# Rows of small matmuls joined in a delta-rule attention and SiLU feed-forward kernel

## The chip, the cores and the metric

The kernel runs on one core of a Trainium2 chip. The metric is the device time of one execution in microseconds (us). Engines: PE (matrix multiply; its weight loads are listed apart as PEld), DVE (vector), ACT (scalar, activations), POOL (general), SP (issues most of the DMAs). Each runs its own queue of instructions in order and waits on semaphores of the others.

## The reference

32 heads (4 batches x 8 heads) of 768 tokens and 48 features go through a delta-rule recurrence; the result, 3,072 tokens of 384 features, goes through a feed-forward block with SiLU.

```
k_n = k / (norm(k) + 1e-6)
state = zeros(48, 48)                       # per batch and head
for t in range(768):
    y[t] = q[t] @ state
    state += beta[t] * outer(k_n[t], v[t] - k_n[t] @ state)
x = y, heads side by side                   # (3072, 384)
h = x @ w_in                                # w_in (384, 2048), given in 64 bits
out = (h * sigmoid(h)) @ w_out              # w_out (2048, 384), given in 64 bits
```

## The kernel before

The tokens are cut into six chunks of 128, c = 0 to 5. Inside a chunk the recurrence is solved as a triangular system per head. For a chunk the work falls into three stages, written as Python generators that are stepped by hand:

- `prepare(c)` (L1431): scale v by the lengths of the keys (`size`, POOL), turn k and q so that their features lie on partitions, then `score(c, b, ...)` for the four batches b. The keys of chunk 2 are turned by `turn` (L501): PE transposes into PSUM (`pt`), DVE copies out. Those of the later chunks and all queries are turned by DVE alone (`turn_blocks`, L489). A score (L530, tile `pa`) is 16 matmuls that write two PSUM banks, of which ACT copies one part and DVE masks the other. After every second score `block_out` has SP store the diagonal blocks of 32x32 to memory (L104, `blocks`), and `block_in` loads them back with one system on each partition.
- `invert(c, step)` (L617 on): DVE inverts the blocks in 31 rounds of two instructions (`rank`, `x`; L628 and L633). `step`, the step size of each token, is made ahead of it by `block_steps` (L442 on): one matmul (`pg`, L446) and an ACT copy. For chunks 2 to 5 the result takes a way through memory and comes back as `xe` and `xi`. For chunk 1 `put_up` (L602) lays it out on the chip instead: two 32x32-block transposes by DVE (into `xe_y` and `up`) and copies of `up` into `xi` and `crossed` by all three engines.
- `solve(c)` (L975): the first merge (L783, `py`, 64 matmuls of 32x32 blocks for both groups of batches), the first keys (L829, `ph`, 32 matmuls), the second merge (`px`), then for each half of the chunk inner and old (L841 and L909), update (L861, `pu`), new (L922, `pyc`), copies of the result to `xT` by ACT, and DMAs (`move`, L902) for those parts that change partition. The second half begins with keys of its own.

Each matmul of the program stands as two PE and two PEld instructions in the profile, a transpose as one of each.

Between these small steps PE works on the feed-forward block of the chunk before. `feed_forward(c, hf)` is also a generator: 16 pieces of `hidden` (L1044, `phid`, six matmul instructions each) and 14 of `combine` (L1151, eight each) for each half of a chunk; chunk 0 has `project` (L1079, `po`) in place of combine. `run(n)` (L1411) takes n such pieces, `go(steps, n)` (L106) n steps of a stage, and `together` (L110) drives several parts matmul by matmul. The order of PE's instructions is the order in which these calls are made; `pin` chains the instructions of every engine in that order. SP's DMAs stand in one line in order of the calls too.

Two places hold the order around the change. Up to the solving of chunk 1 it is a text of words (L1541): s is a step of `solve`, r is `run`, p a step of `prepare(1)`, g makes the step sizes of chunk 1 and the generator of its inversion, i is a round of the inversion, z is a `size` of chunk 1, v loads its v, l and m are steps of the lengths of chunks 1 and 2, f and b narrow the 64-bit weights, t sums weights. From there on it is the loop at L1544: solve chunk c with pieces between its steps, prepare chunk c + 1, invert it with some 23 pieces among its 32 rounds, and take some pieces more.

Of the kernel before, what the change touches and what calls it, by code (L numbers as in the profile page):

```python
# [19 lines left out]
def kernel(  # L20
# [59 lines left out]
    def pin(op):  # L80

        engine = op.ins.engine
        if engine in pins:
            behind(op, pins[engine])
        pins[engine] = op
        return op
# [19 lines left out]
    def go(steps, n=1):  # L106
        for _ in range(n):
            next(steps, None)
# [493 lines left out]
    def put_up(x):  # L602

        both = work.tile([P, BH, T], FP32, name="xe_y", tag="g", bufs=1)
        xes[1], ys[1] = both[:], both[:].rearrange("p (g h) t -> p g h t", g=2)
        pin(nc.vector.transpose(out=both[:].rearrange("p n s -> p s n"), in_=x))
        up = work.tile([P, BH, T], FP32, name="up_1", tag="x", bufs=1)[:]
        pin(nc.vector.transpose(out=up.rearrange("p n t -> p t n"), in_=x.rearrange("p s t -> p t s")))
        for j in (1, 3, 0, 2):
            rows, cols = slice(T * j, T * (j + 1)), slice(T * (j % 2), T * (j % 2) + T)  # L610
            for g in range(2):
                of = up[rows, HH * g : HH * (g + 1)]
                if j % 2 == 1 and g == 1:
                    by_act(crossed[T * (4 - j) : T * (5 - j)], of)
                (by_dve if j % 2 == 1 and g == 0 else by_pool if j % 2 == 0 and g == 0 else by_act)(xis[g][rows, :, cols], of)
# [359 lines left out]
    def solve(c):  # L975

        if c == 0:
            together(inner(0, 0, 0, CC))
            together(inner(0, 1, 0, M))
            yield  # L980
            first_outputs(0)
            yield
            first_outputs(1)
            yield
            together(update(0, 0, 0), update(0, 1, 0))
            yield
            together(keys(0, 0, 1), keys(0, 1, 1))
            yield
            together(inner(0, 0, 1), old(0, 0, 1))
            yield  # L990
            together(inner(0, 1, 1), old(0, 1, 1))
            yield
            together(update(0, 0, 1), update(0, 1, 1))
            yield
            together(new(0, 0, 1), new(0, 1, 1))
            copy_out()
            copy_out()
            move()
            yield
            return  # L1000
        together(merge(c, 0, False), merge(c, 1, False))
        yield
        together(keys(c, 0, 0), keys(c, 1, 0))
        yield
        together(merge(c, 0, True), merge(c, 1, True))
        yield
        for hf in range(2):
            if hf == 1:
                together(keys(c, 0, 1), keys(c, 1, 1))
                if c > 1:  # L1010
                    follow(c)
                yield
            for g in range(2):
                together(inner(c, g, hf), old(c, g, hf))
            if hf == 1:
                if c == 1:
                    follow(c)
                load_v(c + 1)
            yield
            made(c, hf)  # L1020
            yield
            copy_out()
            move()
            if hf == 0:
                yield
# [405 lines left out]
    def prepare(c):  # L1431

        def evacuate(j, e, to, of):
            if j == 1:
                mask(to, of)
            else:
                by_act(to, of)

        def scored(b):
            if b == 0:  # L1440
                block_room(c)
            score(c, b, (0, 1), (A, CC), evacuate)
            if b % HB == 1:
                block_out(c, b // HB)

        if in_blocks(c):
            for g in range(2):
                size(c, g)
            if c == 2:
                for b in range(B):  # L1450
                    turn(c, b, 0, (A, CC)[b % 2], True)
            for g in range(2):
                for b in range(HB * g, HB * (g + 1)):
                    turn_blocks(c, b, 1)
                if g == 1:
                    for b in range(HB):
                        scored(b)
                yield
            for b in range(HB, B):
                scored(b)  # L1460
            block_in(c)
            yield
            return
        block_room(1)
        for b in range(B):
            score(1, b, (0,), (CC, CC), evacuate)
            if b % HB == 1:
                block_out(1, b // HB)
            yield
        block_in(1)  # L1470
        yield
        for b in range(B):
            score(1, b, (1,), (A, CC), evacuate)
            yield
# [63 lines left out]
                pieces = chained(feed_forward(1, 0), feed_forward(1, 1))  # L1538

    for text in (  # L1540
        "s f s f T f q T s q T j5 j4 j8 j8 f j5 f q r T j20 j5 j8 j4 j16 j5 j4 b r q r f j4 j4 f W7 r b j4 f2 j4 j4 j32 r f e j6 j6 b j8 j4 f j4 j20 f j4 r j4 j99 l h f2 b l s w2 f r2 l2 p r s w3 r p r l p f l2 f l3 b l f l2 s l f l p l3 r l3 s l f l r l2 p f s2 l2 f l4 f r2 f p2 v l g r i p i p f r i r i2 r i r i b l i r f r i r b r2 i b b b i2 r2 i2 f b i5 r6 f r f r i2 r2 f r i r f r f i4 f i b r2 i3 b f b f r i r i f k r f r z i b r s r2 t z s b r2 b s m2 r5 t f t m f t m2 r s t m r b s b m r m2 s r m r m r c m2 s m r m t b m2 s m2 b m f m2 t r t m3 r m s m",  # L1541
    ):
        script(text)
    for c in range(1, NCH):  # L1544
        if c > 1:
            solving = solve(c)
            for n in range(9):
                go(solving)
                run(((2, 2, 2, 2, 1, 1, 2, 2, 2), (2, 2, 2, 1, 1, 2, 2, 2, 2))[c == NCH - 1][n])
                if n == 5:  # L1550
                    pieces = chained(pieces, feed_forward(c, 0), feed_forward(c, 1))
        assert next(solving, 0) == 0
        go(long_2, 99)
        if c + 1 < NCH:
            ready = prepare(c + 1)
            go(ready)
            run(2)
            step = block_steps(c + 1)
            for _ in ready:
                run(2)  # L1560
            run(6)
            for n, _ in enumerate(invert(c + 1, step)):
                run(int(n % 4 != 3 and n != 24))
                if n == 3:
                    load_k(c + 2)
                    if in_blocks(c + 2):
                        load_blocks(k, c + 2, ALL)
            after = lengths(c + 2) if c + 2 < NCH else iter(())
            for _ in range({1: 8, NCH - 2: 10}.get(c, 10)):
                run()  # L1570
                go(after, 4)
            go(after, 99)
# [31 lines left out]
```

## Time and profile before

| | us |
|---|---|
| median of 3 runs | 645.06 |
| lowest, highest | 644.01, 648.04 |
| the profiled execution | 643.82 |
| its span, from the first to the last instruction | 642.1 |
| PE busy | 621.8 |
| DVE busy | 404.7 |
| ACT busy | 216.8 |
| POOL busy | 94.8 |

The mean granted clock of PE was 0.978 of full speed. The page cuts the span into 40 slices of 16 us and gives the busy share of each in tenths; the chain of waits is the work that ended last, followed back from the end; "issue" is time in which an engine waited for nothing that the profile shows. A row of a group reads: line, engine, operation, tile written <- tiles read, shapes, count | busy us, mean ns of one | idle us just before them. A row of the timeline reads: start, duration, engine, line, operation, count, and in brackets the idle time before it with what ended it. A row of windows reads: stretch, its length, then for each engine the busy us with the number of instructions, the granted clock, the share of the DMA engines and GB/s.

Large matmuls of the feed-forward block fill most of PE's time: L1044 has 258.5 us, and L1151 has five groups of 28 to 57 us each on the page.

### The profile page before, as it was taken

The page shows a single profiled execution, that of the slowest core. Times are in us where ns is not written, and L with a number is a line of the kernel's source. Part 1 is how long each engine was busy: PE and PEld are TensorE (multiplying, and loading weights), DVE is VectorE, ACT ScalarE, POOL GpSimd, SP SyncE. Part 2 cuts the span into 40 slices and gives each one's busy share as a digit, 9 for nine tenths or more (in the row PEclk, how much of TensorE's full clock was granted, in tenths as well). Part 3 has the DMA queues.
Part 4 walks back from the last instruction along what each step waited for, and adds up shares of the span by engine and source line. Part 5 has one row for each costly group of instructions (what it writes and reads, how often), then busy time and mean ns, then how long its engine had stood idle before and what let it go on. Part 6 is the DMA issues. An engine that isn't in the chain of part 4 may idle for free.

```text
span 642.1 us, 21892 instructions
## 1 busy us (share of the span) xinstructions
PE 621.8 (97%) x9642; PEld 546.6 (85%) x9642; DVE 404.7 (63%) x917; ACT 216.8 (34%) x512; POOL 94.8 (15%) x96
## 2 busy tenths in 40 slices
PE   6879999999999999999999999999999999999997
PEld 4778778666689989989989989989989989889997
DVE  5846879998775974755975554976565963212112
ACT  2656674152251122441122351122451122441120
POOL 5323531255020020020020020020010000000000
PEclk9759999999999999999999999999999999999999
DMA  9756354260469241469142359332163033100101
GB/s 189 168 152 195 109 125 98 74 125 3 101 128 168 43 89 21 86 122 155 39 94 31 75 121 162 57 82 31 46 140 70 22 74 41 40 13 1 26 0 26
DMA packets 141695, 53.69 MB, mean 84 GB/s; under 512 B 113296, under 2 KB 135056, under 8 KB 141600
## 3 DMA queue, kind: packets, MB, share of 16 engines
q1 hardware_dynamic: 141264, 52.14, 39.9%
q8 instruction: 76, 1.25, 0.8%
q10 hardware_dynamic: 336, 0.15, 0.1%
q14 instruction: 19, 0.16, 0.1%
HBM read 39.62 MB, written 10.49 MB: 78 GB/s over the span
## 4 chain that ended last, share of the span: by engine, by line
PE 70%; DVE 10%; DMA 8%; SPq 7%; issue 2%; ACT 1%; POOL 1%; POOLq 0%; DVEq 0%
PE phid L1044 27%; PE px L1151 13%; PE py L1151 10%; PE po L1079 7%; DVE rank L628 4%; DVE x L633 3%; PE pz L841 2%; PE pa L530 2%; SPq L197 2%; PE ph L829 2%; PE pyc L909 2%; SPq L142 1%; PE pyc L922 1%; DVE sums_of_g L1133 1%; DMA up<-x 1%
## 5 line engine op out<-in xcount | busy, mean ns | idle before, releaser
L1044 PE MATMUL phid<-xT,w_in 128*128 128x256 f32 x1152 | 258.5, 382 | 1.0 <-DMA xT<-part 0.9
L1044 PEld LDWEIGHTS phid<-xT,w_in 128*128 128x128 f32 x1152 | 215.8, 190 | 32.0 <-issue 3.0
L1054 ACT ACTIVATE gT<-phid 128x512 f32<-128x512 f32 x88 | 52.5, 598 | 142.2 <-PE phid L1044 137.6
L628 DVE SCALAR_TENSOR_TENSOR rank<-g,step,x 128x31 f32<-128x31 f32 (+15 forms) x124 | 49.7, 401 | 36.5 <-DMA g<-blocks 33.0
L1133 DVE TENSOR_TENSOR sums_of_g<-gT 128x384 f32<-128x384 f32 (+1 forms) x60 | 30.4, 525 | 57.2 <-ACT gT L1054 46.6
L1151 PE MATMUL py<-w_out,sums_of_g 128*128 128x192 f32 x320 | 56.8, 329 | 0.0
L1151 PE MATMUL px<-sums_of_w,sums_of_g 128*128 128x192 f32 x320 | 56.6, 329 | 0.0
L1151 PEld LDWEIGHTS px<-sums_of_w,sums_of_g 128*128 128x128 f32 x320 | 52.2, 190 | 0.5
L1151 PEld LDWEIGHTS py<-w_out,sums_of_g 128*128 128x128 f32 x320 | 52.2, 190 | 0.4
L633 DVE TENSOR_TENSOR x<-x,rank 128x31 f32<-128x31 f32 (+15 forms) x124 | 42.5, 342 | 4.3
L468 POOL TENSOR_TENSOR vf<-vf,n_slot 128x768 f32<-128x768 f32 x10 | 15.2, 1524 | 173.3 <-DMA vf<-in_v_dram 173.3
L868 DVE TENSOR_TENSOR state<-state,pu 48x384 f32<-48x384 f32 x44 | 24.3, 552 | 21.4 <-PE pu L861 20.4
L545 ACT COPY xT<-pyc 48x128 f32<-48x128 f32 (+2 forms) x126 | 32.6, 259 | 1.6
L489 DVE STREAM_TRANSPOSE kq<-stage 128x512 f32<-128x512 f32 x28 | 28.4, 1112 | 5.9 <-DMA stage<-in_q_dram 5.8
L1151 PE MATMUL py<-w_out,gT 128*128 128x192 f32 x160 | 28.4, 329 | 0.0
L1151 PE MATMUL px<-sums_of_w,gT 128*128 128x192 f32 x160 | 28.4, 329 | 0.0
L1151 PE MATMUL px<-w_out,gT 128*128 128x192 f32 x160 | 28.0, 327 | 0.0
L841 PEld LDWEIGHTS pz<-vf,xi 64*64 64x64 f32 x768 | 25.0, 142 | 3.2 <-issue 2.6
L551 POOL COPY g<-x 64x256 f32<-64x256 f32 x4 | 5.0, 1238 | 152.3 <-DVE x L636 152.3
L1151 PEld LDWEIGHTS px<-w_out,gT 128*128 128x128 f32 x160 | 26.4, 190 | 0.5
L841 PE MATMUL pz<-vf,xi 64*64 64x48 f32 x768 | 26.6, 226 | 0.0
L1151 PEld LDWEIGHTS py<-w_out,gT 128*128 128x128 f32 x160 | 26.1, 190 | 0.3
(197 smaller groups left out, 832.3 us busy)
## 6 DMA issues: line engine op xcount, KB each, us to landing
vf<-in_v_dram SPq DMA_DIRECT2D x48, 96.0 KB, 2.9
out_dram<-o SPq DMA_DIRECT2D x42, 96.0 KB, 2.2
w_out<-in_moe_w_in_dram SPq DMA_DIRECT2D x12, 256.0 KB, 3.3
sums_of_w<-in_moe_w_out_dram SPq DMA_DIRECT2D x8, 384.0 KB, 3.6
blocks<-ap SPq DMA_DIRECT2D x40, 64.0 KB, 1.9
g<-blocks SPq DMA_DIRECT2D x5, 512.0 KB, 3.6
kb<-in_k_dram SPq DMA_DIRECT2D x12, 192.0 KB, 4.4
kb<-in_k_dram SPq DMA_DIRECT2D x24, 96.0 KB, 4.5
```

Of the source, the lines that this page charges most:

```text
L468: pin(nc.gpsimd.tensor_tensor(out=vf, in0=vf, in1=of, op=ALU.mult))
L489: pin(nc.vector.transpose(out=kqs[c, b][:, :, j, :].rearrange("p a (i m) -> p a m i", i=T), in_=src.rearrange("p a (m d) -> p a m d", d=D) ...
L545: return pin(nc.scalar.copy(to, of))
L628: pin(nc.vector.scalar_tensor_tensor(out=tv, in0=g[:, 0:m, m : m + 1].to_broadcast([P, m, n]), scalar=step[:, m : m + 1], in1=x[:, m : m + ...
L633: yield pin(nc.vector.tensor_tensor(out=x[:, 0:m, m:T], in0=x[:, 0:m, m:T], in1=tv, op=ALU.add))
L841: yield pin(nc.tensor.matmul(pz[rows, n * D : (n + 1) * D], lhsT=xis[g][rows, u * H + 2 * p + e, :], rhs=vfs[c][rows, hf, g * HB + u, p, : ...
L868: pin(nc.vector.tensor_tensor(out=to, in0=to, in1=by_heads(pu[of]), op=ALU.add))
L1044: pin(nc.tensor.matmul(ph[:, j * GT : (j + 1) * GT], lhsT=w_in[:, a, (2 * f + j) * P : (2 * f + j + 1) * P], rhs=xTs[c, hf][:, a, :], star ...
L1054: pin(nc.scalar.activation(out=hidden_of(c, hf, f), in_=ph[:], func=ACTF.Silu, scale=-0.5 if in_blocks(c) else 0.5))
L1079: pin(nc.tensor.matmul(pos[i][:, 0:DM], lhsT=hidden_of(0, hf, f // 2)[:, at : at + C], rhs=w_outs[f // HFF][:, f % HFF, :], start=(f == 0) ...
L1133: pin(nc.vector.tensor_tensor(out=sums_of_g[:, k, fs], in0=of[0], in1=of[1], op=op))
L1151: pin(nc.tensor.matmul(to, lhsT=at, rhs=quarter(f, *b) if isinstance(b, tuple) else sums_of_w[b][:, f], start=start and f == 0, stop=f == ...
```

## The change

Five edits, all of them in order or layout; no arithmetic is added or taken away.

1. `put_up` (chunk 1): the two transposes write their results without a stride, so that the order of the axes in `xe` and `up` is another; the merge's reads of `xe` and the copies' reads of `up` now have a stride of 32 elements.
2. `solve`: no step ends between the first merge and the first keys. They are issued together, and the loops over `solve` have one step fewer (8, not 9).
3. `prepare` for chunks 2 to 5: the scores of all four batches come in one step, not in two pairs. For chunk 2 a step ends before its keys are turned, so that two pieces come first.
4. In the text for chunk 1: v, l and g (load v, lengths, step sizes) stand ahead of two p (scores), and the second z ahead of the s that holds the first merge.
5. The number of pieces: in the solving of a chunk 2, 2, 2, 1, 1, 2, 2, 2 for all of chunks 2 to 5; after the scores 8; after the inversion 12 (8 where chunk 2 is inverted).

```diff
     def put_up(x):
 
         both = work.tile([P, BH, T], FP32, name="xe_y", tag="g", bufs=1)
-        xes[1], ys[1] = both[:], both[:].rearrange("p (g h) t -> p g h t", g=2)
-        pin(nc.vector.transpose(out=both[:].rearrange("p n s -> p s n"), in_=x))
-        up = work.tile([P, BH, T], FP32, name="up_1", tag="x", bufs=1)[:]
-        pin(nc.vector.transpose(out=up.rearrange("p n t -> p t n"), in_=x.rearrange("p s t -> p t s")))
+        turned = both[:].rearrange("p n t -> p (n t)").rearrange("p (s n) -> p s n", s=T)
+        xes[1], ys[1] = turned.rearrange("p s n -> p n s"), both[:].rearrange("p (g h) t -> p g h t", g=2)
+        pin(nc.vector.transpose(out=turned, in_=x))
+        up = work.tile([P, T, BH], FP32, name="up_1", tag="x", bufs=1)[:]
+        pin(nc.vector.transpose(out=up, in_=x.rearrange("p s t -> p t s")))
...
-                of = up[rows, HH * g : HH * (g + 1)]
+                of = up[rows, :, HH * g : HH * (g + 1)].rearrange("p t n -> p n t")
...
         together(merge(c, 0, False), merge(c, 1, False))
-        yield
         together(keys(c, 0, 0), keys(c, 1, 0))
         yield
...
             if c == 2:
+                yield
                 for b in range(B):
                     turn(c, b, 0, (A, CC)[b % 2], True)
             for g in range(2):
                 for b in range(HB * g, HB * (g + 1)):
                     turn_blocks(c, b, 1)
-                if g == 1:
-                    for b in range(HB):
-                        scored(b)
                 yield
-            for b in range(HB, B):
+            for b in range(B):
                 scored(b)
             block_in(c)
             yield
```

In the text the words around the two places are (before, then after):

```diff
-f r2 f p2 v l g r i p i p f r
+f r2 f v l g p2 r i p i p f r
...
-f r z i b r s r2 t z s b r2 b s m2
+f r z i b r z r2 s t b r2 b s m2
```

And the loop:

```diff
         if c > 1:
             solving = solve(c)
-            for n in range(9):
+            for n in range(8):
                 go(solving)
-                run(((2, 2, 2, 2, 1, 1, 2, 2, 2), (2, 2, 2, 1, 1, 2, 2, 2, 2))[c == NCH - 1][n])
-                if n == 5:
+                run((2, 2, 2, 1, 1, 2, 2, 2)[n])
+                if n == 4:
                     pieces = chained(pieces, feed_forward(c, 0), feed_forward(c, 1))
...
             ready = prepare(c + 1)
+            for _ in range(3 if c == 1 else 2):
+                go(ready)
+                run(2)
+            step = block_steps(c + 1)
             go(ready)
-            run(2)
-            step = block_steps(c + 1)
-            for _ in ready:
-                run(2)
-            run(6)
+            run(8)
...
-            for _ in range({1: 8, NCH - 2: 10}.get(c, 10)):
+            for _ in range(8 if c == 1 else 12):
                 run()
                 go(after, 4)
```

## What I predict

> **What bounds the kernel now.** I read the page first (busy shares, the 40 slices), then the chain of waits in order of time, then the waits of PE, last the DMA queues and counts by window.
>
> ```profile
> PE 621.8 (97%) x9642; PEld 546.6 (85%) x9642; DVE 404.7 (63%) x917; ACT 216.8 (34%) x512; POOL 94.8 (15%) x96
> PE   6879999999999999999999999999999999999997
> PEclk9759999999999999999999999999999999999999
> ```
>
> PE is busy for 621.8 of 642.1 us, at 9 tenths from the fifth slice on and at the full granted clock. The 20 us that it idles lie almost all in the first 50 us, which the change does not touch. So time after that can come from three things only: the cost of each matmul, what PE pays when it goes from one kind of matmul to another, and the few stalls left. The matmuls stay the same ones; only their order changes.
>
> What a switch costs stands in the chain (start, us, what):
>
> ```profile
> 342.33 1.50 PE px L1151 x8
> 343.83 1.30 PE py L1151 x8
> ...
> 451.14 0.86 PE pu L861 x64
> 452.00 0.90 PE pyc L922 x64
> ...
> 563.46 1.04 PE pyc L922 x64
> ...
> 434.43 1.22 PE py L783 x82
> ...
> 438.45 1.08 PE ph L829 x64
> ...
> 471.65 1.91 PE pa L530 x64
> ...
> 476.34 1.91 PE pa L530 x64
> ```
>
> The same eight large matmuls take 1.50 us behind a block of small ones and 1.30 behind large ones: going back costs 0.20. The block "new" (pyc L922) takes 0.90 behind another small block and 1.04 behind large matmuls: going in costs 0.14. The scores (pa L530) take 1.91 both behind the small pg and behind large matmuls, so for them going in costs nothing.
>
> The stalls that PE has in the steady part, each with its releaser in brackets (timeline; the two group rows are of the first merge: chunks 2 to 5, then chunk 1):
>
> ```profile
> 157.74 0.49 PE L922 MATMUL pyc<-ap,z 64*48 64x64 f32 x18 [0.26 <-issue]
> 176.53 0.71 PE L501 MATMUL pt<-ident,kb 128*128 128x128 f32 x5 [0.98 <-issue]
> 341.30 1.03 PE L829 MATMUL ph<-state,kq 48*64 48x48 f32 x56 [0.22 <-issue]
> 548.03 0.33 PE L861 MATMUL pu<-z,kb 64*48 64x48 f32 x10 [0.23 <-issue]
> ...
> L783 PE MATMUL py<-xe,ap 32*32 32x32 f32 x512 | 5.6, 193 | 0.2
> L783 PE MATMUL py<-xe_y,ap 32*32 32x32 f32 x128 | 1.3, 193 | 0.0
> ```
>
> Four of them end with "issue": PE waited for no engine and no transfer. They are the key to this change. Between them lie these numbers of instructions (window, its length, then PE and PEld busy with counts):
>
> ```profile
> q8 instruction: 76, 1.25, 0.8%
> ...
> 157.74:176.53 18.79, 17.81 (x382) 12.93 (x382) 14.40 (x42) 6.80 (x18) 0.00 (x0) 1.00 0.37 87
> 176.53:341.30 164.77, 164.14 (x2033) 150.01 (x2033) 116.29 (x287) 47.42 (x118) 17.07 (x18) 1.00 0.54 95
> 341.30:548.03 206.73, 206.50 (x3306) 189.68 (x3305) 129.89 (x291) 62.00 (x159) 14.00 (x14) 1.00 0.37 72
> ```
>
> One queue carries 76 packets of instructions; PE's 2 x 9642 instructions divided by 76 are 254 a packet. The distances between the stalls are 764, 4,066 and 6,611 instructions: 3 x 254.7, 16 x 254.1 and 26 x 254.3. So PE stalls where a new packet begins, and it does so because the packet isn't there yet. How long a packet takes to come is bounded by the time that the last 254 instructions or so before each stall took:
>
> ```profile
> 154.20:157.73 3.53, 3.27 (x131) 2.26 (x122) 3.24 (x7) 0.53 (x2) 1.48 (x1) 1.00 0.03 5
> 173.50:176.52 3.02, 2.05 (x130) 1.84 (x130) 1.99 (x4) 1.09 (x3) 0.00 (x0) 1.00 0.76 170
> 337.10:341.29 4.19, 3.98 (x132) 3.62 (x118) 3.87 (x15) 1.15 (x2) 0.00 (x0) 1.00 1.06 106
> 544.50:548.02 3.52, 3.29 (x133) 2.90 (x124) 0.00 (x0) 1.34 (x4) 0.00 (x0) 1.00 0.02 5
> ```
>
> 3.0 to 4.2 us, mean 3.6: wherever PE runs through a packet faster than that, it waits for the next. Large matmuls use 16 instructions in 1.3 us and never do. A first merge is 256 instructions in 1.22 us and keys are 128 in 1.08; it is the 2.8 us of large matmuls between them that lets the supply keep up.
>
> **The change part by part.**
>
> *Rows joined.* In chunks 1 to 5 the first merge and the first keys stand together, in chunks 2 to 5 the two pairs of scores. Nine times PE saves going back, 9 x 0.20 = 1.8 us; five times (keys behind the merge) also going in, 5 x 0.14 = 0.7. Sum 2.5 us gained. The row of 0.90 has two blocks of one tile shape behind each other, while a merge has tiles of 32 rows and keys tiles of 48; no row shows that pair, so the term's ends are 2.5 and 1.8 (going back alone), and I take 2.5. [...] What bears on four scores in a row:
>
> ```profile
> 282.33 0.65 ACT L545 COPY ap<-pa 128x256 f32<-128x256 f32 x2 [0.45 <-PE pa L530]
> ...
> 188.14 0.65 ACT L545 COPY ap<-pa 128x256 f32<-128x256 f32 x2 [0.23 <-PE pa L530]
> ...
> 189.51 2.67 SPq L104 DMA_DIRECT2D blocks<-ap  x5
> ```
>
> A score's PSUM banks are used again by the third score behind it; ACT clears them in 0.65 us (two copies) while PE takes 1.91 / 2 = 0.96 for a score, so I cost that at nothing, up to 0.5 a row if an older instruction of ACT or DVE is ahead.
>
> *Stalls that go.* Chunk 2's turned keys (pt) come two pieces later. The packet stall of 0.98 falls there, straight behind update and new; with 2.8 us of large matmuls ahead it goes, for one more switch (0.34): 0.64 gained. Against that, 2.8 us more lie ahead of the scores; the pieces run from the last score to the first merge stay 39 for chunk 2 (8 + 23 + 8) and become 43 in place of 41 for chunks 3 to 5 (the last term 12, not 10). First merges wait today: 5.6 + 0.2 - 4 x 1.3 = 0.6 us over four chunks, for xe. For chunks 3 to 5 two pieces more (2.6 us) hide that; for chunk 2 SP is what sets it (behind the loads of q and v and the moves it comes to the block stores at 189.51, when ACT has cleared the last score at 188.79), and that time stays while the merge comes later. 0.6 gained. In the last chunk two pieces, not one, now stand between inner and update: the 0.23 at 548.03 goes. The 0.22 at 341.30 goes into the next part. Sum 1.7 us gained.
>
> *Waits that come.* In the last chunk one piece fewer stands between "new" and the first hidden of the same chunk:
>
> ```profile
> 549.39 0.56 ACT part L545
> ...
> 553.57 3.56 DMA xT<-part
> ...
> 557.26 1.41 PE L1044 MATMUL phid<-xT,w_in 128*128 128x256 f32 x4 [0.85 <-DMA xT<-part]
> ```
>
> ACT, SP and the DMA need from 549.39 to 557.13 whatever PE does, and PE waits already: one piece of 1.30 less is 1.3 lost. At chunk 1 the step sizes (pg) go ahead of two scores:
>
> ```profile
> 90.24 1.61 ACT L545 COPY xT<-pyc 48x128 f32<-48x128 f32 x6
> 91.91 0.41 PE L446 MATMUL pg<-pick,spread 128*128 128x32 f32 x2 [0.69 <-ACT xT L545]
> ```
>
> pg waits there for a PSUM bank that ACT clears at 91.85. In the new order the second score gets that bank; it is reached at about 91 and the rest of its work comes behind the wait, so 0.3 is lost (ends: 0.7 gained, 0.7 lost). Chunk 1's put_up writes its two turned tiles without a stride and reads them with one. DVE's rows for the same 1,024 elements:
>
> ```profile
> L606 DVE STREAM_TRANSPOSE xe_y<-sums_of_w 128x1024 f32<-128x1024 f32 x1 | 2.0, 2036 | 0.0
> L1294 DVE STREAM_TRANSPOSE sums_of_w<-blocks 128x1024 f32<-128x1024 f32 x1 | 1.2, 1249 | 0.0
> ```
>
> L1294 writes without a stride, so two of them save some 1.5 us of DVE. PE's merge of chunk 1 does not wait (1.3 above) and now comes 2.6 us later, behind two more pieces of large matmuls, so this is worth nothing; a slower strided read of xe by PE costs between 0 and 1.3 (that merge twice as long), and I take 0. Sum 1.6 us lost.
>
> *The packets.* The boundaries lie 254 instructions apart and can be carried from the stalls to the new rows, since both programs have run the same instructions when the first keys of chunks 2 to 5 end. Counts up to those ends:
>
> ```profile
> 176.53:244.36 67.83, 67.49 (x640) 61.38 (x639) 52.57 (x133) 18.19 (x43) 8.59 (x9) 1.00 0.62 106
> 341.30:342.32 1.02, 1.02 (x57) 0.96 (x56) 0.54 (x1) 0.00 (x0) 0.00 (x0) 1.00 0.01 1
> 341.30:439.44 98.14, 98.14 (x1506) 90.16 (x1505) 64.75 (x155) 29.61 (x76) 8.43 (x9) 1.00 0.47 87
> 536.66:548.02 11.36, 11.13 (x353) 10.25 (x350) 5.02 (x10) 3.15 (x8) 0.00 (x0) 1.00 0.02 4
> ```
>
> Chunk 2: 1,279 instructions are 5 packets of 254 and 9 more: one boundary 9 before the end of the keys, the one ahead of it 134 before the end of the merge. Between them 134/256 of 1.22 and 119/128 of 1.08: 1.65 us where 3.6 are needed, so 1.95 lost. Chunk 5: 703 forward to a boundary, three packets (762) back: one 59 before the end of the keys, the other 185 before the end of the merge; 0.88 + 0.58 = 1.46, so 2.1 lost. Chunk 3: one 113 before the end of the keys, the other 239 before the end of the merge, 1.27 us apart; but that first boundary lies only 17 instructions into the merge, and if the sequencer runs that far ahead of PE, its packet is asked for while large matmuls still run. Ends 0.2 (today's stall at this very boundary) and 2.3; I take 0.3, as today's packet, asked for 50 instructions into the merge (254 less 32 large and 16 of the keys leave 206 of its 256), came 0.22 late only. Chunk 4: boundaries 87 before the end of the merge, then 39 behind the keys, then 5 behind the second merge; the first distance takes 0.4 + 1.1 + 2.8 = 4.3, enough, the second 1.2, but the sequencer may enter it earlier: between 0 and 2.4, I take 0.7. Chunk 1's boundaries lie as in chunk 4 with longer pieces: 0. A row of scores is 256 instructions in 3.8 us: 0. Sum 5.1 us lost (ends 3.0, with packets in 3.0 us and nothing in chunks 3 and 4, and 9.5, with 4.2).
>
> *The sum.* -2.5 - 1.7 + 1.6 + 5.1 = +2.5 us. The profiled execution took 643.82 (642.1 of span and 1.7 around it), so 646.3. That run lies 1.2 under the median of 645.06, inside the spread of the three (644.01 to 648.04); I predict **646.3** and let the range carry the difference.
>
> **The rivals.** *The supply keeps up* (25%): in the new order packets are asked for far enough ahead, and only the mean of small and large matters. Against it: four stalls at whole packets. For it: these four cost 1.7 us in all, and today's rows of update and new are 256 instructions in 1.8 us and stall rarely. Time: 643.82 - 2.5 - 1.7 + 1.6 = 641.2. *Every row starves* (7%), the side of slower: packets take 4.2 us or more whenever PE takes small matmuls without a break, so each of five merge-and-keys rows loses 2.5 and each of four score rows 0.5, with 0.4 for what follows each of the nine: 12.5 + 2.0 + 3.6 = 18.1 in place of 5.1, 659.3; it decides from about 10 us of packet stalls on, at which the whole is over 1% slower. [...]
>
> **How the numbers follow.** 60% for the forecast, whose own range is 643.8 to 649.5 (the packets' ends in part, the pg bank, the run-to-run spread). From 641.2 less some noise of a run to the strided case and some starving: 640.3 to 650.5 for eight in ten. A measurement of this kernel can tell about 1%, 6.5 us. Faster by more than that (under 638.6) needs the first rival and all gains at their ends: 0.03. Slower (over 651.5): starving, and a little of the strided case: 0.09. Within 1%: 0.88.
>
> **What would show it.** New PE stalls that end with "issue", near 2 us each, inside the first keys of chunks 2 and 5, and none of that length in chunk 1; the 0.98 ahead of pt gone; phid in the last chunk waiting about 2.2 us for xT; runs of 1.50 us fewer by nine. If the keys run through in 1.1 us behind the merge everywhere, the packet term is wrong and the first rival holds; if scores stall too, the second.

## The result and the profile after

The changed kernel takes 655.92 us (median of 6 runs, 655.35 to 657.32) where the kernel before, timed beside it, takes 646.09 (6 runs, 644.01 to 648.23): a ratio of 1.0153, 95% interval 1.0124 to 1.0182. It is 9.8 us slower, 9.6 above the forecast and 5.4 above the upper end of the range. The profiled execution took 655.94 with a span of 654.1.

The page of the changed kernel, in its rows for PE and its clock:

```profile
span 654.1 us, 21891 instructions
...
PE 627.6 (96%) x9642; PEld 554.4 (85%) x9642; DVE 404.0 (62%) x917; ACT 220.1 (34%) x512; POOL 95.6 (15%) x96
...
PE   6879999999999998999999999999999998899997
...
PEclk8759999999999997999999999999999998899999
```

The span grew by 12.0. PE has the same 9,642 instructions, yet is busy for 5.8 us more, and idle for 6.2 more. Idle time was forecast; that the same instructions take longer was not. The clock row tells where: a 7 in slice 16 and 8s in slices 34 and 35, where before stood 9s.

Not all of the 12.0 belongs to the change. Before the first product of the last projection of chunk 0 (`po`) stand some 115 us in which loading and start-up vary from kernel to kernel, also where nothing was edited: in the experiments that do not add instructions there, the first `po` comes between 115.37 and 120.60. Of the change, only the first move of edit 4 (loads, lengths and step sizes of chunk 1) lies ahead of it: scores (pa) wait there for ACT for 1.02 + 0.35 us where pg waited 0.69 before, 0.7 more. The forecast had 0.3 for that, 0.7 at its end. The timeline has that first `po` before, then after the change:

```profile
115.62 1.76 PE L1079 MATMUL po<-w_out,gT 128*128 128x384 f32 x4
```

```profile
118.24 0.81 PE L1079 MATMUL po<-w_out,gT 128*128 128x384 f32 x2
```

From there to the end it is 642.1 - 115.6 = 526.5 before and 654.1 - 118.2 = 535.9 after: 9.4 us. This stretch, called the rest below, is compared in the experiments; everything that the change does from chunk 1's first merge on lies in it. Each "rest" comes from the one execution that was profiled. PE's busy time in it, before and after (windows):

```profile
115.62:642.11 526.49, 519.97 (x7161) 461.31 (x7159) 317.50 (x711) 152.90 (x375) 52.09 (x46) 1.00 0.37 70
118.24:654.14 535.90, 524.43 (x7161) 467.65 (x7159) 316.61 (x710) 155.86 (x375) 52.87 (x46) 0.99 0.36 69
```

So of the 9.4 us, 4.5 are longer busy time and 4.9 are idle time.

The timeline of PE in the first keys of chunk 2, then of chunk 5 (start, us, what, idle time before it with its releaser):

```profile
243.60 0.25 PE L784 MATMUL py<-xe,ap 32*32 32x32 f32 x4
244.37 1.25 PE L784 MATMUL py<-xe,ap 32*32 32x32 f32 x124 [0.51 <-DMA xe<-low]
245.55 1.13 PE L830 MATMUL ph<-state,kq 48*64 48x48 f32 x61
249.15 0.45 PE L830 MATMUL ph<-state,kq 48*64 48x48 f32 x3 [2.46 <-issue]
...
541.44 0.78 PE L830 MATMUL ph<-state,kq 48*64 48x48 f32 x35
544.26 0.76 PE L830 MATMUL ph<-state,kq 48*64 48x48 f32 x29 [2.04 <-issue]
```

The two stalls stand where the packet count had put them, in those two rows and with about that length (1.95 and 2.1 were forecast). What follows them is new. Windows of the changed kernel (length, PE and PEld busy with counts, DVE, ACT, POOL, then the granted clock, DMA share, GB/s):

```profile
243.50:249.15 5.65, 2.65 (x191) 2.30 (x190) 5.14 (x18) 1.16 (x2) 0.00 (x0) 0.88 1.07 122
249.15:255.00 5.85, 5.85 (x44) 5.48 (x47) 1.02 (x2) 0.06 (x1) 0.00 (x0) 0.54 0.02 3
255.00:262.00 7.00, 7.00 (x278) 6.68 (x264) 2.91 (x5) 2.93 (x7) 0.00 (x0) 1.00 0.02 5
...
544.30:550.50 6.20, 6.20 (x173) 5.84 (x173) 2.47 (x5) 0.33 (x1) 0.00 (x0) 0.72 0.01 3
...
565.50:569.50 4.00, 2.35 (x6) 1.00 (x6) 0.63 (x2) 0.17 (x1) 0.00 (x0) 0.89 0.36 86
569.50:572.70 3.20, 3.20 (x130) 3.13 (x129) 0.00 (x0) 0.53 (x2) 0.00 (x0) 0.61 0.28 67
```

Behind each standstill PE runs without a gap, but at 0.54, 0.72 and 0.61 of its clock in the mean of these windows. Length times missing clock is 5.85 x 0.46 + 6.20 x 0.28 + 3.20 x 0.39 = 2.7 + 1.7 + 1.2 = 5.6 us, and up to 0.4 more in the window ahead of the third (0.89). That is more than half of the 9.4. It is also more than the 4.5 of longer busy time, because the joined rows save more busy time than chunk 1 (below) pays. The loss in the third of these windows stands behind the waits of the last chunk's first hidden for xT:

```profile
565.98 0.67 PE L1044 MATMUL phid<-xT,w_in 128*128 128x256 f32 x2 [0.67 <-DMA xT<-part]
567.02 0.67 PE L1044 MATMUL phid<-xT,w_in 128*128 128x256 f32 x2 [0.38 <-DMA xT<-part]
568.49 1.10 PE L1044 MATMUL phid<-xT,w_in 128*128 128x256 f32 x2 [0.80 <-DMA xT<-part]
```

Chunk 1 pays as well. Groups of the changed kernel (busy us, mean ns | idle): the merge of chunk 1 and three of the copies of `up`:

```profile
L784 PE MATMUL py<-xe_y,ap 32*32 32x32 f32 x128 | 2.0, 228 | 0.0
...
L545 ACT COPY xi<-up 32x512 f32<-32x512 f32 x4 | 4.3, 1073 | 0.0
...
L551 POOL COPY xi<-up 32x512 f32<-32x512 f32 x2 | 2.8, 1402 | 0.1
L548 DVE COPY xi<-up 32x512 f32<-32x512 f32 x2 | 2.3, 1132 | 0.1
```

Reading with a stride makes the merge 2.0 instead of 1.3 us; the copies, by the same group rows before, took 616 (ACT), 776 (POOL) and 570 ns (DVE).

### The profile page after: what moved, and what is told of

Read it like the earlier page. It is cut to its first block, busy times and chain, and to the rows that moved or that the text cites. A ratio compares the mean times of both kernels' runs of the same rounds, so it can differ in the third digit from the quotient of the medians.

```text
span 654.1 us, 21891 instructions
## 1 busy us (share of the span) xinstructions
PE 627.6 (96%) x9642; PEld 554.4 (85%) x9642; DVE 404.0 (62%) x917; ACT 220.1 (34%) x512; POOL 95.6 (15%) x96
## 3 DMA queue, kind: packets, MB, share of 16 engines
q8 instruction: 76, 1.25, 0.8%
## 4 chain that ended last, share of the span: by engine, by line
PE 81%; DMA 7%; SPq 5%; DVE 3%; issue 2%; ACT 2%; POOL 0%; POOLq 0%; DVEq 0%
PE phid L1044 34%; PE px L1151 16%; PE py L1151 12%; PE po L1079 6%; PE pa L530 3%; SPq L142 2%; DMA w_out<-in_moe_w_in_dram 2%; PE pz L842 2%; PE pyc L910 2%; PE pyc L923 2%; PE ph L830 1%; PE pu L862 1%; DVE rank L629 1%; PE py L784 1%; DMA sums_of_g<-in_q_dram 1%
## 5 line engine op out<-in xcount | busy, mean ns | idle before, releaser
L1151 PE MATMUL px<-sums_of_w,gT 128*128 128x192 f32 x160 | 30.5, 347 | 0.0
L1151 PEld LDWEIGHTS px<-sums_of_w,gT 128*128 128x128 f32 x160 | 28.6, 204 | 0.1
```

The source lines that it names most:

```text
L1151: pin(nc.tensor.matmul(to, lhsT=at, rhs=quarter(f, *b) if isinstance(b, tuple) else sums_of_w[b][:, f], start=start and f == 0, stop=f == ...
```

## The experiments

Theory: two packet boundaries of the joined rows fall where PE has little work left, PE stands still for over 2 us, and a standstill of that size also brings the clock down for the next 4 to 6 us. Rivals: the joined rows cost time wherever the boundaries lie; the strided reads; the scores in one row; the clock falls for a reason of its own.

Below, "rest" is the time from the first `po` to the end in the profile, 526.5 for the kernel before and 535.9 for the changed one.

**Boundaries moved a little.** The changed kernel with 26 repeated 32x32 matmuls near its start, which write the same blocks again:

```diff
     first_blocks(2)
+    first_blocks(2, 26)
     beta_of(0)
```

> The changed kernel with 26 more small matmuls (104 PE instructions) in the first stage, which write the same blocks of chunk 0 a second time; all that follows stands in the same order, but 104 instructions further on in the stream. If the two stalls of 2.5 and 2.0 us in the first keys of chunks 2 and 5 are waits for a packet of 254 instructions, they go (under 0.5 us each) and stalls of 1.8 to 2.5 us with the same releaser (issue) come up in the first keys of chunks 1 and 4, with the granted clock near half in the large matmuls behind them; the time stays within 3 us of the changed kernel. If the keys wait there for data (state, lengths of keys, a PSUM bank) because the merge no longer has large matmuls behind it, the stalls stay in chunks 2 and 5.

659.3 us, 1.018 of before (1.0119 to 1.0241); rest 536.5. The stall of chunk 5's first keys is gone, and others have come in the joined rows of chunks 1 and 4 (1.03 and 1.85, where 1.8 to 2.5 were expected). Timeline of PE:

```profile
147.20 0.68 PE L830 MATMUL ph<-state,stage 48*64 48x48 f32 x31 [1.03 <-issue]
...
252.17 1.74 PE L830 MATMUL ph<-state,kq 48*64 48x48 f32 x55 [1.53 <-issue]
253.84 4.44 PE L1151 MATMUL px<-sums_of_w,gT 128*128 128x192 f32 x14
...
452.27 1.09 PE L830 MATMUL ph<-state,kq 48*64 48x48 f32 x29 [1.85 <-issue]
453.30 3.87 PE L1151 MATMUL py<-w_out,sums_of_g 128*128 128x192 f32 x15
```

In PE's instruction stream the stalls of this kernel in chunks 1, 2 and 4 begin at instructions 5,526, 8,322 and 14,174 (PE and PEld counted together): 11 x 254.2 and 23 x 254.4 apart. So they belong to the packets and not to a chunk. Chunk 2 keeps a stall, since the boundary is now 18 instructions into the keys and the one ahead of it lies in the merge, which itself waits 0.72 us for xe; that its packet is asked for late for that reason is likely but not shown. The time does not fall, because clock is lost here too: 14 large matmuls take 4.44 us. In chunk 2 the clock is at half from 250.91 on, 0.27 us into the stall of 1.53, so the wait of 0.72 ahead of it may have a part in that; no run shows it apart.

**Rows apart again.** Edits 2 and 4 undone, with the order of pieces that goes with them (the last chunk's too); the strided tiles and the scores in one row stay:

```diff
         together(merge(c, 0, False), merge(c, 1, False))
+        yield
         together(keys(c, 0, 0), keys(c, 1, 0))
```

> The changed kernel with edits 2 and 4 undone: large matmuls stand between first merge and first keys again, in chunk 1 with the old text, while the layout of edit 1 and the scores in one row and later turned keys of edit 3 stay. Packets: no PE stall over 1 us after the first 100 us except ahead of xT, granted clock 1.00 through all solving, time 8 to 11 us under the changed kernel, 643 to 648. If the layout or the scores' row cost most of the loss, the time stays above 650.

647.78 us, 1.0013 of before (0.9983 to 1.0043); rest 527.6. So 8.3 of the 9.4 us hang on the joined rows and what was reordered for them. One packet stall over 1 us is left, 1.27 in a hidden at 182.16, behind update and new; the clock stays at 1.00. At the very boundary of chunk 2 the wait is now 0.15, behind 2.9 us of large matmuls:

```profile
245.67 2.87 PE L1152 MATMUL px<-w_out,gT 128*128 128x192 f32 x16
248.47 1.13 PE L830 MATMUL ph<-state,kq 48*64 48x48 f32 x60
249.76 0.32 PE L830 MATMUL ph<-state,kq 48*64 48x48 f32 x4 [0.15 <-issue]
```

**Tiles without a stride.** Edit 1 undone, all else as changed.

> The changed kernel with edit 1 undone (chunk 1's turned tiles without a stride where they are read). If the strided reads cost what the profile of after shows in chunk 1 (first merge 2.00 us in place of 1.29, and the copies of up 1.07, 1.13 and 1.40 us in place of 0.62, 0.57 and 0.78, which let the DMA of xT come late by 0.7), the time falls by 0.7 to 1.5 us: the merge is back at 1.3 and phid of chunk 1 no longer waits 0.7 for xT. The stalls in chunks 2 and 5 stay at 2 to 2.5 us. If the layout were the main loss, 5 us or more go.

656.81 us, 1.0129 (1.0047 to 1.0211). Chunk 1's merge takes 1.3 us again (2.0 with the stride), and the wait of chunk 1's first hidden for xT goes from 0.68 to 0.49. The stalls of chunks 2 and 5 are still there (2.41 and 1.88) with their clock, and the rest (536.8) shows no gain; in the last chunk the clock stayed at half for 6.8 us where it was 3.4 in the changed kernel, which hides it. The strided reads cost the merge about 0.7 us and do not decide.

**Scores in two pairs.** Edit 3's scores undone in the changed kernel.

> The changed kernel with the scores of chunks 2 to 5 in two pairs with two large pieces between them (8 pieces behind the first pair as before: 2 and 6). Position in the stream of all first merges stays, so the stalls in chunks 2 and 5 stay. If joining the scores saves going back to large matmuls, four times 0.2 us, the span grows by 0.8 to 1.4 us; if the row of 256 small instructions costs by itself, the time falls by more than 1 us.

657.3 us, 1.0158 (1.0092 to 1.0225); rest 537.0, 1.1 more than the changed kernel, with stalls of 2.56 and 1.86 in place. The scores in one row are not what went wrong. What they are worth this pair of traces doesn't tell: here the last chunk waits 1.07 + 0.49 + 0.77 us for xT and keeps its clock, where the changed kernel lost it.

**Stalls put in by hand.** The kernel before, with nothing of the change. In the middle of nine combines a matmul waits for a row of 1 to 5 ACT copies; its product is overwritten:

```diff
+GAPS = (1, 3, 2, 4, 3, 1, 4, 2, 5, 0)
...
+        def hold():
+            held = kept[:].rearrange("p k m -> p (k m)")[:, 0:DM]
+            for _ in range(gap):
+                pin(nc.scalar.copy(held, px[:, 0:DM]))
+            pin(nc.tensor.matmul(py[:, left], lhsT=held[:, 0:P], rhs=held[:, HM:DM], start=True, stop=True, skip_group_check=True))
```

> The kernel before, with nothing of the change, and nine stalls of PE put in by hand: in the middle of nine combines one 128x192 matmul waits for a row of 1, 2, 3, 4 or 5 ScalarE copies of 128x384 (0.49 us each in the trace of before) that start when PE's last product is there. No packet and no block of small matmuls is near. Theory (any standstill of PE of about 2 us or more brings the granted clock down): stalls of about 0.7, 1.2, 1.7, 2.2 and 2.7 us, 14 us in all; behind the two of 2.2 and the one of 2.7 the granted clock falls to 0.5 to 0.7 over the next 5 us and the next 16 large matmuls take 4.5 to 5.3 us in place of 2.87; behind those of 0.7 and 1.2 nothing. Time 643.8 + 14 + 3 x 2.5 = 665.3, a little more if the stalls of 1.7 cost clock too. Rival (the slow matmuls behind the new stalls come from the row of small tiles ahead of them, not from the standstill): no loss of clock anywhere, 658.

668.51 us (one run). The timeline of five of the nine, each with the idle time before it:

```profile
250.94 0.59 PE L1152 MATMUL py<-kept 128*128 128x192 f32 x2 [1.64 <-ACT kept L1151]
354.42 0.59 PE L1152 MATMUL py<-kept 128*128 128x192 f32 x2 [2.15 <-ACT kept L1151]
410.92 0.59 PE L1152 MATMUL py<-kept 128*128 128x192 f32 x2 [1.63 <-ACT kept L1151]
510.76 0.66 PE L1152 MATMUL py<-kept 128*128 128x192 f32 x2 [2.14 <-ACT kept L1151]
609.14 0.59 PE L1152 MATMUL py<-kept 128*128 128x192 f32 x2 [2.65 <-ACT kept L1151]
609.57 4.44 PE L1160 MATMUL py<-w_out,sums_of_g 128*128 128x192 f32 x16
```

The windows that follow them, with the granted clock third from the right:

```profile
250.94:253.94 3.00, 3.00 (x132) 2.71 (x133) 0.62 (x1) 0.98 (x3) 0.00 (x0) 0.63 0.00 0
354.42:357.42 3.00, 3.00 (x138) 2.77 (x138) 0.00 (x0) 0.34 (x1) 0.00 (x0) 1.00 0.00 0
410.92:413.92 3.00, 3.00 (x18) 3.00 (x19) 2.79 (x8) 0.34 (x1) 0.00 (x0) 1.00 1.21 149
510.76:513.76 3.00, 3.00 (x10) 3.00 (x11) 2.76 (x8) 0.34 (x1) 0.00 (x0) 0.57 0.00 0
609.14:612.14 3.00, 3.00 (x12) 3.00 (x13) 0.56 (x1) 0.34 (x1) 0.00 (x0) 0.67 0.00 0
```

With no packet and no joined row, a standstill alone (those of 2.14 and 2.65) brings the clock down: 16 large matmuls take 4.44 us in place of 2.87. Behind the one of 1.64 a second merge follows within 1 us, so that one is not as clean. But the rule in the expectation was too simple. Of two stalls of 2.14 and 2.15 the first lost clock and the second not, and the same holds for 1.64 and 1.63; the four of 0.57 to 1.13 lost none. Three lost, as forecast, though not the three named. The time came 3 us above the forecast.

**Boundaries moved out of the way.** As the first experiment, with 35 repeated matmuls.

> The changed kernel with 35 repeated 32x32 matmuls (140 instructions of PE, 0.7 us) ahead of the first merge of the program, so that every later packet boundary lies 140 instructions earlier in the program; all rows stay joined. Carried forward by packets of 254 to 256, the boundaries then leave the first keys of chunks 2 and 5: stalls of 1.0 to 1.2 us and 0.5 to 0.7 around the first merge of chunk 3 and 1.1 to 1.3 us in the first keys of chunk 4, none over 1.3 us, and no loss of clock but that of the last chunk's xT wait. Theory (stall plus clock): the time from the first po to the end falls from 535.9 to about 530.5, the total to about 651. Rival (the joined rows themselves cost the time, wherever the boundary lies): 536 and 656 to 657.

The rest falls to 529.6, by 6.3 us, with every row still joined. Some 1.8 of it is not the boundaries' doing: the last chunk waits 0.45 + 0.80 us for xT, 0.6 less than in the changed kernel, and keeps its clock (1.2). The timeline of chunk 2's row, then the only stall over 0.5 us in a row of chunk 4:

```profile
250.99 1.25 PE L784 MATMUL py<-xe,ap 32*32 32x32 f32 x124 [0.50 <-DMA xe<-low]
252.17 1.15 PE L830 MATMUL ph<-state,kq 48*64 48x48 f32 x64
253.25 2.87 PE L1151 MATMUL px<-sums_of_w,gT 128*128 128x192 f32 x16
...
449.54 0.91 PE L830 MATMUL ph<-state,kq 48*64 48x48 f32 x47 [0.66 <-issue]
```

Keys without a gap, and behind them 16 large matmuls in 2.87, though the merge had waited 1.13 + 0.50 us for xe. Chunk 5's row has none either, chunk 3 stalls of 0.63 and 1.25, about as forecast. The rival of the costly rows falls: 536 was its forecast. The total, though, is 655.66 (1.0176, 1.014 to 1.0212): the first `po` comes at 123.76, since the repeats themselves make two stalls at the start:

```profile
14.74 0.81 PE L1292 MATMUL blocks<-kq 48*32 48x32 f32 x62 [2.87 <-issue]
...
21.00 0.61 PE L446 MATMUL pg<-pick,spread 128*128 128x32 f32 x2 [4.40 <-issue]
```

The second of these is new (in the kernel before, pg came at 15.46): pg comes 5.5 us later, not the 0.7 of the expectation.

**One piece back in the last chunk.**

```diff
-                run((2, 2, 2, 1, 1, 2, 2, 2)[n])
+                run(((2, 2, 2, 1, 1, 2, 2, 2), (2, 2, 1, 1, 2, 2, 2, 2))[c == NCH - 1][n])
```

> The changed kernel, but in the last chunk one of the two pieces ahead of update stands behind new again, as before the change. Theory: the waits of phid for xT in that chunk fall from 0.67 + 0.38 + 0.80 to the one wait of about 0.85 that the kernel before had, the granted clock stays at 1.00 there, and the inner and old blocks behind take 2.1 us again in place of 3.2: 1.0 + 1.9 = about 2.9 us less from the first po to the end (533.0), total about 653. Rival (the waits cost only themselves): 1.0 to 1.3 us less, the matmuls behind as slow as in the changed kernel. The stalls in the keys of chunks 2 and 5 stay.

654.11 us, 1.0121 (1.009 to 1.0152). The first hidden waits once, for 0.40, and the 130 instructions of inner and old behind it run at full clock:

```profile
569.30:571.40 2.10, 2.10 (x130) 2.05 (x130) 0.00 (x0) 0.53 (x2) 0.00 (x0) 1.00 0.61 146
```

3.20 us at 0.61 in the changed kernel, 2.10 at 1.00 here: the clock loss there came from the waits. The rest is 534.8, only 1.1 less instead of 2.9: chunk 5's keys stalled for 2.01, about as in the changed kernel, but this time the half clock behind them lasted 6.8 us where it was 3.4.

**Only the scores in one row and the later turned keys** (all rows apart, tiles and step sizes as before), and **the same with chunk 1's row joined and its step sizes ahead**:

> Of the change only the scores in one row (chunks 2 to 5) and the later turned keys of chunk 2; first merge and first keys apart in every chunk, chunk 1's tiles and step sizes as before. Theory: no stall of a packet over 1.3 us, no loss of clock; against the kernel with both joins undone the strided tiles go too (0.7 in the merge of chunk 1), so from 527.6 to about 526.7 from the first po on, beside 526.5 before: 4 x 0.34 gained by the scores and about as much given back by waits for xe in chunks 2 and 4 (0.71 and 0.49 there) and a packet of 1.28 where 0.98 was. Total within 0.3% of before. Rival (the scores in a row and the later turn are worth their 1.4 + 0.6 in full): 524.5, total about 643.

> As the kernel with the scores in one row, and in addition merge and keys joined in chunk 1 and chunk 1's step sizes ahead of two scores, the two parts of the change in which no packet boundary was seen to hurt. Theory: one way back to large matmuls (0.20 to 0.34) less, the wait of the step sizes gone from pg and back in pa: 526.4 from the first po on, total the same as the kernel with the scores in one row to 0.3%. Rival (merge and keys in one row cost time wherever they stand, for example by the strided or late tiles of chunk 1): a new stall over 1 us in the first keys of chunk 1 and 528 or more.

644.36 us, 0.9975 of before (0.9951 to 1.0000), rest 527.1; and 646.75, 1.0025 (1.0003 to 1.0047), rest 527.0. In neither profile has the clock fallen behind the first `po`. In the first, PE's busy time there is 0.7 us less than before (519.24, 519.97), near the 4 x 0.20 that the prediction gave to four rows of scores, and waits give it back (idle 1.3 more), most of all the merges of chunks 2 and 3 for xe (timeline of the first kernel, chunk 2):

```profile
239.16 1.25 PE L783 MATMUL py<-xe,ap 32*32 32x32 f32 x124 [0.78 <-DMA xe<-low]
```

The first of the two is the best version found; its 1.1 us are hardly more than its uncertainty. (Another mix of these parts took 655.17 us. In it the steps of chunk 1's solving came one too early against the rest, so that chunk 1 was computed from other data and PE stood still for 4.75 us there; its time says nothing on the question. But its chunk 2, with rows apart, lost clock behind waits of 0.57 and 0.81 for xe.)

**All causes out, rows joined**: 35 repeats, the last chunk's piece, tiles without a stride.

> All rows joined as in the changed kernel, but each cause found so far taken out: packet boundaries moved by 35 repeated 32x32 matmuls, the last chunk's piece back behind new, chunk 1's two tiles as before. Theory: from the first po to the end 535.9 - 6.3 (boundaries, as measured) - 1.1 (last chunk, as measured) - 1.4 (strided reads) = 527.1, near the 526.5 of before; the total is 5 to 6 us more than that suggests, since the repeated matmuls were seen to cost 5.6 us at the start of the program: about 651 to 653. Rival (a cause is missing from the list): 529.5 or more from the first po on.

654.81 us, 1.0122 (1.0081 to 1.0163), rest 529.2: between the two. No stall over 1 us is left behind the first `po`, yet the clock fell twice, in chunk 2 behind waits of 0.31 and 0.81 for xe, and in chunk 4:

```profile
447.89 0.91 PE L829 MATMUL ph<-state,kq 48*64 48x48 f32 x47 [0.73 <-issue]
448.73 4.55 PE L1150 MATMUL py<-w_out,sums_of_g 128*128 128x192 f32 x16
```

0.73 us cost clock here where 0.66 at the same instruction did not in the experiment with 35 repeats. Each loss makes 16 matmuls 1.6 to 1.7 us longer, 3.3 in all. So a cause was missing from the list, and it was the clock again: in a joined row a short stall can be enough. Nor is the loss the same in every execution: of the six of this kernel one took 648.55 at a mean granted clock of 0.979, the others 653.75 to 655.42 at 0.968 to 0.971.

## Why the prediction was wrong

The step that failed is the one that priced the packets, "so 1.95 lost" and "so 2.1 lost". It took a stall to cost its own length, with PE at full clock behind it. Its place and its cause were right and its length nearly; the half clock behind it was missing from the sum, 5.6 us of the 9.4. The evidence at hand was the 0.98 in chunk 2, behind which the clock stayed at 1.00; a stall of double that length was priced in proportion. The first four slices of the clock row (9759) showed that the clock can fall; the prediction read it from the fifth slice on.

Point by point, from the first `po` on:

- *Packets*, +5.1 forecast: 2.46 + 2.04 in chunks 2 and 5, 0.2 in chunk 4, nothing in chunk 1 and hardly anything in chunk 3 (its keys took 0.13 longer): 4.8. Right in the two main places (4.5 for 4.05); that the sum fits so well is luck, since chunks 3 and 4 gave 0.3 for 1.0.
- *Clock*, not in the sum: 2.7 in chunk 2's solving, 1.7 in chunk 5's first keys and 1.2 behind the later waits for xT in the same chunk, the last.
- *Waits that come*, +1.6: the hidden of the last chunk waits for 0.67 + 0.38 + 0.80 in place of 0.85, 1.0 more where 1.3 was forecast. "A slower strided read of xe by PE costs between 0 and 1.3, and I take 0": 0.7. Inside the range given for it, wrong as a value; the copies did not hold the second merge up, but chunk 1's first hidden waits 0.68 for xT, a wait that was not foreseen. It isn't tied to the strides: without them it is 0.49 in one kernel and 0.78 in another (all causes out), and with them it is 0.18 where the scores stand in two pairs. Its cause stays open.
- *Stalls that go*, -1.7: the 0.98 ahead of pt and the 0.23 in the last chunk are gone, but chunk 2's merge waits 0.51 for xe, and first merges with their waits take 5.4 + 0.5 us where it was 5.6 + 0.2: nothing of the 0.6 came. For chunk 2 the argument was that SP's time stays while the merge comes later. SP's time did not stay: it came to the block stores 73.9 us behind the first `po` before and 76.0 after (189.51 and 194.24 in the two timelines).
- *Rows joined*, -2.5: keys behind a merge start 1.08 us ahead of what follows (252.17 to 253.25 in the experiment with 35 repeats), exactly what they took behind large matmuls. So nothing is saved going in, and the term is 1.8 at most, its lower end.
- *The rivals*: "the supply keeps up" is refuted by the two stalls; "every row starves" came near the time (659.3), but by the wrong way, since only two of nine rows stalled. The range reached 650.5 because no case held a price for a stall beyond its length. The strided case that it runs to is shown by no run: the traces have 0.7 more in chunk 1's first merge and no wait of PE ahead of the second.

By these the sum is 2.5 + 5.6 (clock) + 0.7 (merge) + 0.7 (chunk 1's hidden) + 0.7 (joins) + 0.7 (xe) - 0.3 - 0.3 (packets and the last hidden, which were smaller) = 10.3 where 9.4 was measured, so it is good to about 1 us. For busy time alone it closes: 5.6 + 0.7 - 1.8 is the 4.5 of the two windows. The experiments carry its two largest parts: boundaries moved, 6.3 us less with the rows joined, some 4.5 of it theirs; rows apart, 8.3 less.

What stays open is when exactly a stall costs clock. Behind the first `po` of all these kernels but the mix, 11 of 12 stalls of 1.85 us and over cost it, as did 2 of 3 from 1.5 to 1.7. Of the shorter ones those put in by hand among large matmuls did not (up to 1.13), nor did the packet stalls of 1.27 (rows apart) and 1.2 (only the scores in one row) behind update and new, while some in or close ahead of a merge and keys did (0.73, 1.03, and 0.31 with 0.81).

The traces say more than these lengths. In narrow windows the granted clock is 1.00 or 0.50, and it changes only in steps: in the changed kernel at 247.74, 254.57, 544.70, 548.11, 568.60 and 572.01, which are 2, 85, 1, 6 and 1 steps of 3.413 us apart (324.27 us are 95). Here are one such step of the changed kernel with the stretch behind it, then one of the kernel with stalls by hand with the step behind it:

```profile
244.33:247.74 3.41, 2.32 (x185) 2.16 (x186) 3.04 (x13) 1.16 (x2) 0.00 (x0) 1.00 1.42 150
247.74:254.57 6.83, 5.42 (x19) 5.26 (x18) 2.38 (x4) 0.00 (x0) 0.00 (x0) 0.50 0.04 6
...
350.74:354.15 3.41, 1.53 (x12) 1.23 (x8) 1.02 (x2) 1.70 (x4) 0.00 (x0) 1.00 0.00 0
354.15:357.57 3.42, 3.15 (x139) 2.89 (x140) 0.00 (x0) 0.62 (x3) 0.00 (x0) 1.00 0.00 0
```

In the first step PE idles 1.09 us and works on a merge and keys, and half clock follows; it begins 1.05 us into the stall of 2.46, with the rest of that stall still to come. In the other PE idles 1.88 between large matmuls, and the clock stays. So how long PE stood still doesn't decide alone: the step with a merge and keys lost clock at 1.09 us of idle time, the one with large matmuls kept it at 1.88. Whether the 0.66 and the 0.73 differ in the same way isn't shown: behind the 0.73 the clock falls at 448.97, so the step ahead of that begins at 445.56, in the merge; around the 0.66 the clock is 1.00 from 445.90 to 453.00, and nothing there tells where a step begins. Scores without a stall cost nothing: of the step from 189.71 to 193.13 in the changed kernel 3.1 us are scores (189.07 to 192.80), and the clock stays at 1.00 behind it. This is read across kernels; no run changed the tiles alone, so that a merge and keys count for less than large matmuls is the author's estimate, and the limit isn't known.

## What to carry to other kernels

A stall of PE can have a second price: look at the granted clock behind it. Here it was half speed for 3.4 or 6.8 us behind all but one of the stalls of 1.85 to 2.65 us, and behind 1.03 and 0.73 in rows of tiny matmuls. Such rows ran through a packet of instructions faster than the next one came: 256 instructions of a merge take 1.22 us and 128 of keys 1.08, where the 254 ahead of each of the four stalls of before had taken 3.0 to 4.2. Count instructions from a stall in the trace, in steps of 254 here, before joining two such rows, and leave a few us of large matmuls between them (behind 2.9 us of them the wait at chunk 2's boundary was 0.15, behind the bare merge 2.46). The 26 and 35 matmuls added far ahead moved the later boundaries, and so the price of the same reorder: with all rows joined the rest was 536.5, 535.9 or 529.6 by the boundaries' place, beside 526.5 before. Judge it by the stall's position, not by its look.

## What the hardware showed

Two stalls of 2.14 and 2.15 us, made in the same way in one run, cost 1.7 us or nothing. What tells them apart in the trace is their place among the steps of 3.413 us: the first lies whole in one step (507.75 to 511.16, where the clock falls); the second is split at 354.15, 46 steps ahead of 511.16, into 1.88 and 0.27. That the place decides is the author's estimate from this pair. The pair of 1.63 and 1.64 isn't explained by it, since each lies whole in one step; the step that lost clock ends with 0.3 us of a merge. Stalls of 1.64 and, but for that one of 2.15, of 1.85 to 2.65 us cost clock, and in a joined row once 0.73.

With 35 repeated 32x32 matmuls at the start, below 1 us of work, pg came at 21.00 in place of 15.46, behind a stall of 4.40 that ends with issue, and the first `po` at 123.76 in place of 118.24. And fp32 reads with a stride of 32 elements cost ACT 1,073 ns in place of 616 for a copy of 32x512, DVE 1,132 in place of 570, POOL 1,402 in place of 776, and PE's merge of chunk 1 2.0 in place of 1.3 us.
